# One core, attention with random features and an MLP: ones matmuls pinned to TensorE's front, queue order and PSUM banks searched anew

## The chip, the cores and the metric

The kernel runs on one core of one Trainium2 chip. The metric is the device time of one execution in microseconds (us), all phases included; less is better. PE is the matmul engine (TensorE), DVE the vector engine, ACT the scalar engine, POOL GpSimd, and SP the engine that here does nothing but issue transfers. Each engine works through its own queue in a fixed order, and waits on semaphores for the others.

## The reference

Two parts, one after the other. Attention works on 64 pairs of batch and head with 576 positions of 64 numbers and 128 features; the MLP works on the 4608 rows that come out of it.

```
q_s, k_s = q * scale, k * scale                      # q, k, v: 8 x 8 x 576 x 64
phi(x): h = x @ omega.T - sum(x*x)/2
        return exp(h - max(h)) / sqrt(128)           # 576 x 128
q_p, k_p = phi(q_s), phi(k_s)
kv  = k_p.T @ v                                      # 128 x 64
z   = sum over positions of k_p
out = (q_p @ kv) / (q_p @ z + 1e-6)
x   = out as 4608 x 512                              # heads side by side
h   = x @ w_in                                       # 512 x 2048
y   = (h * sigmoid(h)) @ w_out                       # 2048 x 512
```

## The kernel before

**Windows of attention.** The 64 pairs are taken two at a time, in 32 *windows*, numbered 0 to 31. A window loads its keys and queries (`load_raw` and `load_nat`, lines L420 to L430) and values (`load_v`, L434). PE projects them on omega: `project` (L465 for windows 0 to 3, L470 for 4 to 7, L474 for the rest) and `project_mid`, `project_mids` for the middle rows (L486, L488, L493). In windows 0 to 3 the projection also reads the squares of the inputs, which ACT makes (`square_raw`, L448). DVE takes maxima (L503, L505, L509) and makes of them the shifts `nb` and `nbm` (L512, L513); exponentials are made on ACT (L533, L538) with parts of the subtraction on DVE (L545, L549, L554, L556). PE makes `kv` (L599), turns it (`kv_turn`, L607), sums the keys to `z` (L591); DVE makes the denominators (`denom`, L623, L629); POOL divides (`normal`, L634, and by DVE at L586 for windows 9 to 11).

**Two ways to turn the queries.** The divided features have to be transposed before the last product `numer` (L678). In 17 windows PE does it (`turn`, L657, copied by ACT at L661). In the 15 windows of `CROSS` (13 to 15 and 20 to 31) a transfer does it: ACT splits the words into two planes of 16 bits (`planes`, L642), SP issues a DMA transpose (`cross`, L646), and ACT joins the planes again (`words`, L651).

**The MLP.** Every product of the MLP is one helper, `thrice` (L848): a high and a low part of each operand, three matmuls. Weights are prepared once, kept in device memory and loaded from there in pieces `w` (512 KB; L830, L835, L840, L844) into a ring of seven buffers; operands `ts` are split into a high part by ACT (L890) and a low part by DVE (L894); sums of results are DVE's (`deep_add`, L940; `c_add`, L967), with results stored from `c` at L970 and L973. POOL makes sums and low parts of weights (L762, L781, L789, L812). MLP products begin while attention still runs; from about 580 us on PE has hardly anything else.

**What sets the order.** All work is recorded as *units* by `add(name, engine, ...)`, 3649 of them, and issued in one global order that a table of numbers gives, `RANK`, one number per unit. An engine's queue is its own units in that order. PSUM has three pools, `att` (2 banks), `acc` (4) and `h` (2); a second table, the string `HOMES`, says from which pool each unit of PE takes its banks.

```
    def run(self):
        order = sorted(zip(RANK, self.units.values()), key=lambda x: x[0])
        homes, done = iter(HOMES), set()
        for _, u in order:
            assert done.issuperset(u["after"]) and done.issuperset(u["order"]), u["name"]
            u["pools"] = [{"a": "att", "c": "acc", "h": "h"}[next(homes)] for _ in range(u["banks"])]
```

A transfer thus stands where `RANK` puts it in SP's queue, and everything behind it in that queue waits until SP has issued it. One unit computes nothing that is used: `warm` (L397) multiplies a tile of ones with itself, eight matmuls of 128x128, into a bank of its own. It waits for the tile of ones alone, which DVE writes at L385.

```
    def warm(ps):
        for _ in range(WARM):
            nc.tensor.matmul(ps[:, :P], ones.bitcast(F32), ones.bitcast(F32), start=True, stop=True)
    add("warm", "PE", 3.4, -9, warm, banks=1, free=[bk("warm")])
```

Of the kernel before, what the change touches and what calls it, by code (L numbers as in the profile page):

```python
# [39 lines left out]
BOTH = tuple(range(22, 32))  # L40
# [100 lines left out]
class Plan:  # L141
# [221 lines left out]
def attention_mlp(ctx: ExitStack, tc: tile.TileContext, qX, kX, qS, kS, qT, kT, qn, kn, v, om_in, w_in, w_out, out):  # L363
# [635 lines left out]
    for n in range(NWIN):  # L999
        calm = n < LEAD  # L1000
        fold = n in FOLD
        rows = {}
        for i, who in enumerate("kq"):
# [4 lines left out]
            def prev(s):  # L1008
# [3 lines left out]
                order=prev("raw") + ([("raw", n, "k")] if i else [("raw", n - 1, "q")] if n else []), alloc=[("in", ("in",) + w)], lat=1.1)  # L1012
# [4 lines left out]
            else:  # L1017
                before = [("nat", n, "k")] if i else ([("nat", n - 1, "q")] if n and n - 1 not in FOLD else [])
                add(("nat",) + w, "SP", 0.42, at(n, i - 13.5, 8.1 + 10 * i - 32), lambda n=n, who=who: load_nat(n, who),
                    order=before + [("raw",) + w], lat=0.95)  # L1020
# [564 lines left out]
```

## Time and profile before

| what | before |
|---|---|
| device time, median of 3 runs | 944.0 us (943.92, 944.0, 946.3) |
| the profiled execution: its time, and the span from first to last instruction | 945.41 us, 943.6 us |
| PE busy | 923.0 us (98%) |
| DVE busy | 736.3 us (78%) |
| ACT busy | 679.8 us (72%) |
| POOL busy | 384.1 us (41%) |
| mean clock granted to PE | 0.999 |
| bytes moved | 245.14 MB |

The time of an execution is 1.8 us more than the span of the profiled one. A share of busy time is a mean over the whole span, and PE's 98% leaves 20.6 us in which it does nothing: before the first matmul, in waits, and after the last.

### The profile page before, as it was taken

The numbers are of one execution on the slowest core, as the hardware profiler recorded it, in microseconds if no ns is written. First come the engines' busy times: TensorE is split into PE (matmuls) and PEld (weight loads), VectorE is DVE, ScalarE is ACT, GpSimd is POOL, SyncE is SP. The second block draws the span as 40 slices with busy tenths as digits, with TensorE's granted clock in tenths as the row PEclk, the third lists the DMA queues.
The fourth block names the chain that finished last, engine by engine and source line by source line (L and its number), as shares of the span: only waits on it lengthen the run. The fifth ranks groups of instructions, "written<-read, shape, count | busy, mean of one in ns | idle before, by whom it ended". The sixth has DMA issues, their size and how long they took to land.

```text
span 943.6 us, 16346 instructions
## 1 busy us (share of the span) xinstructions
PE 923.0 (98%) x5577; PEld 747.7 (79%) x5577; DVE 736.3 (78%) x1633; ACT 679.8 (72%) x1199; POOL 384.1 (41%) x430
## 2 busy tenths in 40 slices
PE   7999999999999999999999999999999999999998
PEld 6888887877778777777877877778878887888886
DVE  5887775797766698768998998898999974468865
ACT  7998895668987876888699897886667555114642
POOL 3775666785868556756233234322120210000000
PEclk9999999999999999999999999999999999999999
DMA  7769899998899998859968578897766575567662
GB/s 245 206 221 357 295 345 332 308 350 266 313 321 311 309 360 250 312 197 345 327 221 303 160 266 258 264 263 257 217 199 202 184 262 192 198 209 238 214 222 90
DMA packets 138258, 245.14 MB, mean 260 GB/s; under 512 B 48704, under 2 KB 79552, under 8 KB 138176
## 3 DMA queue, kind: packets, MB, share of 16 engines
q1 hardware_dynamic: 138176, 244.10, 77.7%
q8 instruction: 45, 0.74, 0.3%
q14 instruction: 37, 0.30, 0.1%
HBM read 191.17 MB, written 44.04 MB: 249 GB/s over the span
## 4 chain that ended last, share of the span: by engine, by line
PE 85%; ACT 6%; DVE 4%; DMA 3%; issue 1%; POOL 0%; SPq 0%; DVEq 0%; ACTq 0%; POOLq 0%
PE ps_acc L848 56%; PE ps_h L848 13%; PE ps_att L599 2%; ACT f L538 2%; PE ps_h L474 1%; PE ps_att L678 1%; PE ps_acc L474 1%; PE ps_att L474 1%; DMA out<-c 1%; DMA f<-f 1%; PE ps_acc L599 1%; PE ps_acc L465 1%; PE ps_att L470 1%; PE ps_acc L678 1%; DVE prod L623 1%
## 5 line engine op out<-in xcount | busy, mean ns | idle before, releaser
L848 PE MATMUL ps_acc<-ts,w 128*128 128x512 f32 x2544 | 597.6, 392 | 3.2 <-DVE ts L894 1.2
L848 PEld LDWEIGHTS ps_acc<-ts,w 128*128 128x128 f32 x2544 | 472.3, 188 | 104.4 <-DVE ts L894 2.0
L894 DVE TENSOR_TENSOR ts<-g,ts 128x1024 fp32r<-128x1024 f32 x112 | 144.2, 1297 | 38.7 <-ACT ts L890 38.5
L890 ACT CAST ts<-g 128x1024 fp32r<-128x1024 f32 x112 | 117.2, 1058 | 76.5 <-PE ps_acc L848 65.6
L848 PE MATMUL ps_h<-xq,w 128*128 128x512 f32 x576 | 141.1, 394 | 0.0
L848 PEld LDWEIGHTS ps_h<-xq,w 128*128 128x128 f32 x576 | 106.1, 188 | 21.4
L940 DVE TENSOR_TENSOR g<-ps_acc,g 128x512 f32<-128x512 f32 x144 | 93.6, 682 | 24.1 <-PE ps_acc L848 23.6
L634 POOL TENSOR_TENSOR f<-f,rd 128x384 f32<-128x384 f32 x87 | 82.8, 975 | 63.6 <-DVE rd L629 51.2
L568 POOL TENSOR_TENSOR t<-hk 128x256 f32<-128x256 f32 x64 | 48.8, 778 | 141.3 <-ACT hk L538 73.1
L886 DVE TENSOR_TENSOR g<-g,g 128x1024 f32<-128x1024 f32 x64 | 79.2, 1256 | 0.2
L582 POOL TENSOR_TENSOR es<-t,es 128x256 fp32r<-128x256 f32 x32 | 29.3, 914 | 86.0 <-ACT es L578 85.3
L762 POOL TENSOR_TENSOR w<-g,w 128x512 fp32r<-128x512 f32 x32 | 42.8, 1347 | 32.4 <-ACT w L758 23.4
L944 ACT ACTIVATE g<-g 128x1024 f32<-128x1024 f32 x36 | 37.2, 1056 | 16.4 <-DVE g L940 16.3
L623 DVE CUSTOM_DVE_ANT_0 prod<-f,ps_att 128x128 f32<-128x128 f32 (+1 forms) x130 | 37.1, 286 | 14.4 <-PE ps_att L591 6.0
L651 ACT COPY f<-f 128x2304 uint16<-128x2304 uint16 x15 | 42.5, 2835 | 4.2 <-DMA f<-f 4.2
L574 POOL TENSOR_TENSOR t<-t,hk 64x128 f32<-64x128 f32 x64 | 37.4, 584 | 14.2 <-ACT hk L533 10.1
L967 DVE TENSOR_TENSOR c<-ps_acc,c 128x512 f32<-128x512 f32 x48 | 31.6, 683 | 14.1 <-PE ps_acc L848 12.4
L623 DVE CUSTOM_DVE_ANT_0 prod<-f,ps_acc 128x128 f32<-128x128 f32 (+1 forms) x110 | 31.4, 286 | 11.8 <-ACT ic L816 4.7
L906 ACT CAST ts<-xq 128x1024 fp32r<-128x1024 f32 x21 | 22.1, 1058 | 25.0 <-PE ps_acc L848 23.4
L443 DVE TENSOR_REDUCE sq<-in 128x9 f32<-128x576 f32 x48 | 34.9, 738 | 3.1 <-ACT in L438 3.1
L910 DVE TENSOR_TENSOR ts<-xq,ts 128x1024 fp32r<-128x1024 f32 x21 | 26.2, 1246 | 14.2 <-ACT ts L906 14.2
L474 PE MATMUL ps_att<-oms,in 64*128 64x128 f32 x280 | 35.9, 279 | 0.9 <-ACT f L538 0.8
(208 smaller groups left out, 1535.6 us busy)
## 6 DMA issues: line engine op xcount, KB each, us to landing
w<-w_d SPq DMA_DIRECT2D x168, 512.0 KB, 5.4
w<-ws_d SPq DMA_DIRECT2D x48, 512.0 KB, 4.5
v<-v SPq DMA_DIRECT2D x32, 320.0 KB, 5.5
out<-c SPq DMA_DIRECT2D x17, 512.0 KB, 5.1
in<-kT SPq DMA_DIRECT2D x24, 352.0 KB, 5.6
g<-w_in SPq DMA_DIRECT2D x16, 512.0 KB, 5.5
g<-w_out SPq DMA_DIRECT2D x16, 512.0 KB, 6.1
w_d<-w SPq DMA_DIRECT2D x16, 512.0 KB, 6.5
```

Of the source, the lines that this page charges most:

```text
L474: nc.tensor.matmul(ps[:, cols], T["raw", n, who][r, o : o + P], oms[r], start=True, stop=True)
L568: nc.gpsimd.tensor_tensor(t[:, i], e[:, 5 * i : 5 * i + 2], e[:, 5 * i + 2 : 5 * i + 4], ALU.add)
L574: nc.gpsimd.tensor_tensor(t[r, i - 3, 0], t[r, i - 3, 0], e[r, MID], ALU.add)
L623: nc.vector.tensor_tensor_reduce(out=prod[r], in0=e[r, c], in1=z[r, j * M : (j + 1) * M], scale=1.0, scalar=GUARD, op0=ALU.mult, op1=ALU.a ...
L634: nc.gpsimd.tensor_tensor(e[:, c], e[:, c], rd[:, c].unsqueeze(2).broadcast_to([P, 3, M]), ALU.mult)
L651: nc.scalar.copy(en.bitcast(U16).rearrange("p (n b) -> p b n", b=2), halves)
L762: nc.gpsimd.tensor_tensor(lo, T["w", i], hi.bitcast(F32), ALU.subtract)
L848: nc.tensor.matmul(ps, w(a), x[:, b], start=first and n == 0, stop=last and n == 2, **more)
L886: nc.vector.tensor_tensor(out, a, b, ALU.subtract)
L890: nc.scalar.copy(g[:, 0], T["g", p, SOURCE[j], u])
L894: nc.vector.tensor_tensor(g[:, 1], T["g", p, SOURCE[j], u], g[:, 0].bitcast(F32), ALU.subtract)
L940: nc.vector.tensor_tensor(to, T["q", p, chain, i], T["g", p, r, i // 2][:, i % 2], ALU.add)
```

## The change

It has three parts. The unit `warm` becomes something that the first two projections must follow (`order`), so that its matmuls stand at the front of PE's queue. All of `RANK` is another table, and so is `HOMES`. Operations, their number, their sizes and the buffers stay as they were; 15 windows still go by a DMA transpose.

```
 RANK = (
-    (one number for each of 3649 units)
+    (other numbers for the same units)
...
 HOMES = (
-    "chaccchccaachcacchcahchaccchchcchcachcahccacccahccaachccacccacchacccccachcaaaaaaahhhaaaahahaaaahahaa"
+    "caccchachcahcccchaacacchhacchcchcahccchcacccccahachccchachcaccchccccacachahaaaaaahahhhaaahaaaaahahaaa"
...
                 add(pj, "PE", 2.0 if n in BESIDE else 1.7 if fold else 0.99, at(n, 3 * i, o),
                     lambda a, b, n=n, who=who: project(n, who, a, b), banks=2, after=pj_after,
-                    order=([("proj", n - 1, "k" if n - 1 in BOTH else who)] if n else []) + ([("mids", n)] if i and not fold else []),
+                    order=([("proj", n - 1, "k" if n - 1 in BOTH else who)] if n else ["warm"]) + ([("mids", n)] if i and not fold else []),
```

**PE, the start of the program.** Before, the first rows of PE's queue are the projection of window 0's keys (the tiles: `in` holds inputs and their squares, `omr` is omega):

```order
L1578 UNCONDITIONAL_BRANCH
L465 MATMUL ps_acc<-omr,in 128x128
L465 MATMUL ps_h<-omr,in 128x128
L465 MATMUL ps_acc<-ones,in 128x128
L465 MATMUL ps_h<-ones,in 128x128
```

and `warm` stands far behind, between a middle projection of windows 4 to 7 (L488) and the turns of an earlier window:

```order
L470 MATMUL ps_att<-omn,in 128x128
L488 MATMUL ps_acc<-omn,in 128x128
L397 MATMUL ps_acc<-ones 128x128 x8
L607 MATMUL ps_acc<-ident,kt 128x128
L657 MATMUL ps_att<-ident,f 128x128 x3
L657 MATMUL ps_h<-ident,f 128x128 x3
```

After, the queue begins with it:

```order
L1578 UNCONDITIONAL_BRANCH
L397 MATMUL ps_acc<-ones 128x128 x8
L465 MATMUL ps_att<-omr,in 128x128
L465 MATMUL ps_acc<-omr,in 128x128
L465 MATMUL ps_att<-ones,in 128x128
L465 MATMUL ps_acc<-ones,in 128x128
```

The eight matmuls have moved from behind some 150 rows to the first place, and the projection takes its banks from other pools.

**SP, the transpose of window 14.** Before (L434 loads values, L708 is a store of results' rest, L801, L830 and L844 load weights, L794 stores weights):

```order
L708 DMA rest_96<-xr 128x64
L801 DMA ic<-w_d 128x1024
L794 DMA w_d<-c 128x2x256 x2
L434 DMA v<-v 128x640
L646 DMA_TRANSPOSE f<-f 128x18x128
L844 DMA w<-w_d 128x1024 x3
L434 DMA v<-v 128x640
L844 DMA w<-w_d 128x1024 x2
```

After:

```order
L434 DMA v<-v 128x640
L708 DMA rest_95<-xr 128x64
L801 DMA ic<-w_d 128x1024 x2
L844 DMA w<-w_d 128x1024 x6
L646 DMA_TRANSPOSE f<-f 128x18x128
L426 DMA in<-qT 128x576
L430 DMA in<-kn 128x576
L826 DMA ws_d<-ic 128x2x256 x2
```

Six loads of weights that came right behind the transpose, or later, now stand right ahead of it; behind it stand inputs of a later window.

**POOL, around window 11's maxima.** Before (`es` are sums of keys' features, `t` their parts, `g` and `c` weights):

```order
L568 TENSOR_TENSOR t<-hk 128x256 x2
L570 TENSOR_TENSOR t<-t 128x2x128
L574 TENSOR_TENSOR t<-t,hk 64x128 x2
L789 TENSOR_TENSOR c<-g_1292,c 128x512 x2
L781 TENSOR_TENSOR g_1440<-g_1440 128x256
L582 TENSOR_TENSOR es<-t,es 128x256
L781 TENSOR_TENSOR g_1440<-g_1440 128x256 x3
```

After:

```order
L568 TENSOR_TENSOR t<-hk 128x256 x2
L570 TENSOR_TENSOR t<-t 128x2x128
L781 TENSOR_TENSOR g_1344<-g_1344 128x256 x3
L789 TENSOR_TENSOR c<-g_1344,c 128x512 x2
L781 TENSOR_TENSOR g_1450<-g_1450 128x256 x3
L574 TENSOR_TENSOR t<-t,hk 64x128
L781 TENSOR_TENSOR g_1450<-g_1450 128x256
L574 TENSOR_TENSOR t<-t,hk 64x128
```

The same kinds of operations stand in another order, and six sums of weights (L781) and two low parts (L789) now come between the second and the third step of the keys' sums.

## Rows read from the trace of the kernel before

**Rows 1.** The page's part 1, and PE's granted clock in 40 equal slices (tenths).

```profile
PE 923.0 (98%) x5577; PEld 747.7 (79%) x5577; DVE 736.3 (78%) x1633; ACT 679.8 (72%) x1199; POOL 384.1 (41%) x430
...
PEclk9999999999999999999999999999999999999999
```

**Rows 2.** What PE waited for: total us, times, longest us.

```profile
PE ps_acc L591 <- DVE hk L556: 1.6, 1, 1.6
...
PE ps_acc L848 <- DVE ts L894: 1.2, 1, 1.2
PE ps_acc L657 <- DVE hk L545: 1.1, 1, 1.1
PE ps_acc L848 <- DMA w<-w_d: 0.9, 1, 0.9
PE ps_acc L599 <- DMA v<-v: 0.8, 1, 0.8
...
PE ps_h L678 <- ACT f L651: 0.4, 1, 0.4
```

**Rows 3.** Busy time by stretch: PE, PEld, DVE, ACT, POOL; clock; DMA.

```profile
24.00:48.00 24.00, 22.07 (x231) 18.88 (x231) 21.42 (x85) 22.16 (x54) 17.03 (x25) 1.00 0.79 211
48.00:72.00 24.00, 23.89 (x179) 20.31 (x180) 20.64 (x71) 23.35 (x56) 16.95 (x21) 1.00 0.71 228
...
580.00:938.00 358.00, 357.85 (x1814) 291.19 (x1813) 279.70 (x476) 200.42 (x240) 40.34 (x49) 1.00 0.66 215
```

**Rows 4.** PE's timeline at the start: start us, duration, instruction, [idle before].

```profile
4.83 0.58 PE L465 MATMUL ps_acc<-omr,in 64*128 64x128 f32 x1 [4.83 <-ACT omr L403]
...
5.41 0.42 PE L465 MATMUL ps_acc<-ones,in 64*128 64x128 f32 x1
...
5.63 0.42 PE L465 MATMUL ps_acc<-ones,in 64*128 64x128 f32 x1
...
8.54 0.79 PE L486 MATMUL ps_att<-omr,in 128*128 128x128 f32 x2
...
11.68 0.27 PE L465 MATMUL ps_acc<-omr,in 64*128 64x128 f32 x1
```

**Rows 5.** ACT's timeline, the squares of window 1's keys.

```profile
8.14 0.74 ACT L448 ACTIVATE in<-in 128x640 f32<-128x640 f32 x1 [1.47 <-DMA in<-kX]
```

**Rows 6.** DVE's timeline at the start.

```profile
0.83 0.17 DVE L385 MEMSET ones<- 128x128 f32 x1 [0.83 <-PEq L1572]
...
11.92 1.29 DVE L505 TENSOR_REDUCE nbk<-ps_acc 128x4 f32<-128x512 f32 x2 [1.23 <-PE ps_acc L465]
...
27.93 0.69 DVE L505 TENSOR_REDUCE nbq<-ps_acc 128x4 f32<-128x512 f32 x1 [0.93 <-PE ps_acc L465]
```

**Rows 7.** PE's timeline from 40 to 49 us, the unit `warm`.

```profile
40.99 1.95 PE L397 MATMUL ps_acc<-ones 128*128 128x128 f32 x16
```

**Rows 8.** Line L646: ns min/median/max on SP, and from issue to landing.

```profile
L646 SPq DMA_TRANSPOSE f<-f x15: 1773/2246/5782, 289.5 to 763.9; - x15
...
DMA to landing us min/median/max: 3.9/5.1/8.9
```

**Rows 9.** SP's timeline, the transpose of window 14.

```profile
314.73 5.78 SPq L646 DMA_TRANSPOSE f<-f  x1
```

**Rows 10.** The chain that ended last: start us, us, what.

```profile
206.14 3.90 DVE nbm L512
...
320.62 4.32 DMA w<-w_d
...
343.25 9.18 DMA out<-c
...
563.47 8.90 DMA f<-f
```

**Rows 11.** Tile nbm, one group: ns min/median/max, first and last start.

```profile
L512 DVE TENSOR_TENSOR nbm<-mxm,sq x24: 144/161/3892, 145.5 to 708.5; 128x2 f32<-128x2 f32 x24
```

**Rows 12.** Busy time from 206.14 to 210.03 us, columns as in rows 3.

```profile
206.14:210.03 3.89, 3.89 (x18) 3.00 (x17) 3.89 (x1) 1.07 (x2) 3.87 (x5) 1.00 1.03 384
```

**Rows 13.** Busy time from 310 to 320 us, same columns.

```profile
310.00:320.00 10.00, 10.00 (x45) 8.27 (x45) 4.16 (x6) 9.97 (x16) 3.57 (x3) 1.00 1.07 288
```

More of the change, by code (lines that the diff above doesn't have):

```diff
@@ L169 @@
 RANK = (
[183 rows of a table removed]
[183 rows of a table added]
 )
 HOMES = (
-    "chaccchccaachcacchcahchaccchchcchcachcahccacccahccaachccacccacchacccccachcaaaaaaahhhaaaahahaaaahahaa"
-    "haahaahhhaacchhacccccaacccaachaccaccacchchacaccachhccaccacacaaccacchaccaachcchcaacahaccacacaahahhcac"
-    "cahhcahchahahchcahcahchaccahaahahaaahahccaahcahccchahaahahcchccahhahahaccchhahcaachahcahahcacaaahaha"
-    "hhachcachcaahcchhchaachchaacacchahacahhcahcahhahaahahchacahhchacachaaahhch"
+    "caccchachcahcccchaacacchhacchcchcahccchcacccccahachccchachcaccchccccacachahaaaaaahahhaaahaaaaahahaaa"
+    "aahahahhhaahccahcacaacccacaccaccaaaccacchcaccccacacchcacccaccachahcahcaacccccaaacacachcacacaaaaahhaa"
+    "ahahhacahcahhahcahhaccahhhhaahahahahhaacchahcahccchahahcahachccahhahahacchahaachacaahhahahcacacahaha"
+    "hachcaachcaahchchhhaachchaachcahchaaahhahacaahahaahahchahahchaaccchhahahac"
 )
```

366 rows, old and new, of the table RANK are left out of this document.

## The prediction

> **What bounds the kernel now.** I read the page first. PE is busy 923.0 us of the span of 943.6, DVE 736.3 and ACT 679.8, and PE's granted clock shows 9 tenths or more in every slice [rows 1]. The change adds no work to PE and takes none away: the same units, the same shapes, 15 windows still turned by a transfer. So PE's 923.0 us stay, and what can move is the 20.6 us in which PE does nothing. I took those apart by the list of PE's waits and its timeline. Before the first matmul PE sits 4.83 us, until omega is there [rows 4]; after its last matmul some 4.3 us pass with the last sums and the store. The other 11.4 us are waits between, and the six that the change can touch are in [rows 2]: 1.6 and 1.1 for DVE's subtractions, 1.2 for low parts, 0.9 for a load of weights, 0.8 for values, 0.4 for a joined transpose.
>
> Then the stretches. From 24 to 48 us PE is busy 22.07 of 24, ACT 22.16, DVE 21.42: no engine alone is the bound, the three wait for each other. From 48 to 72 PE is busy 23.89 and ACT 23.35 [rows 3]. What comes earlier in the first 48 us therefore comes earlier at the end, if PE has no gap later that swallows it, and from 580 us on PE has 0.15 us of gaps [rows 3].
>
> One more fact is hidden in PE's 923.0: a slow start. The first projection's steps follow each other every 0.22 us (5.41, 5.63); it takes from 4.83 to 8.54, 3.71 us [rows 4]. The same work at full pace takes 1.88 us (the next one, from 11.68 on). The unit `warm` takes 0.12 us for each of its 16 passes at 41 us [rows 7], so the first projection ran at half that pace, as at 1.2 of the two levels 1.2 and 2.4 GHz, although the slices of [rows 1] show full clock. The half pace ended at about 9.2 us, after PE had worked without a gap since 4.83.
>
> **The change, step by step. First: `warm` to the front.** It needs only the tile of ones, which DVE has written at 1.0 [rows 6]. At half pace 16 passes take 16 x 0.22 = 3.5 us, so it is done by about 4.6, before omega is there at 4.83: it costs nothing there. At 41 us it leaves a hole of 1.95 us of PE's time [rows 7]. And the slow start falls on it: of the 4.4 us that PE worked at half pace before (4.83 to 9.2), 3.5 are now `warm`'s, and some 0.9 are left for the first projection, which then takes about 2.2 us instead of 3.71: 1.5 us earlier. (If the pace does not rise by then, the projection stays at 3.7.)
>
> Not all of that arrives. Window 1's keys are squared by ACT at 8.14 only, when their load lands [rows 5], and are ready at 8.88; their projection takes 1.88 at full pace, and so ends at about 10.8 instead of 11.68: 0.9 us. This is the part I hold for certain, as DVE works without a break from that point (11.92, [rows 6]) and it and ACT feed PE. Two waits inside this stretch may go besides, since the queues around them are in another order: DVE's 0.93 at 27.93 [rows 6] and PE's 0.8 for values [rows 2], whose load now stands earlier in SP's queue, ahead of a weight load. I count three quarters of these 1.75, 1.3 us. **Head: -2.2.** Bounds: 0, if DVE and ACT stay the bound with their own order; -6.1, if PE were it (1.95 for `warm`, 2.2 of half pace, and the 1.93 that PE lacks from 24 to 48 us, [rows 3]).
>
> **Second: transposes and the loads around them.** A transpose holds SP between 1.77 and 5.78 us, and lands 3.9 to 8.9 us after its issue [rows 8]. The long ones are those issued while other transfers fly. That of window 14 holds SP from 314.73 to 320.5 [rows 9]; the loads of weights behind it are issued from 320.62 on, the first lands 4.32 us later [rows 10], and PE waits 0.9 for it [rows 2]. The transpose at 563.47 takes 8.90 [rows 10], and PE waits 0.4 for its words. The wait of 1.2 for low parts goes back along the chain to a store that took 9.18 us at 343.25 [rows 10], in traffic, not to a transpose.
>
> After, six loads stand ahead of window 14's transpose, and PE has some 20 us of work between it and the first product that needs a load behind it, against 2 before. That removes the 0.9. The joined words now have about twice the work ahead of their user (median over the 15 windows, by durations of before), so the 0.4 should go too, and the 1.2 depends on a ring of `c` that comes round in another order: half of it. That is -1.9. On the other side, windows 20, 27 and 30 have 0 to 4 us of PE's work (again by durations of before) between their transpose and the first load needed behind it; a hold of 2.25 (the median) and a landing of 4.3 do not fit into that if the ring is not full. Before, seven windows were as tight and one of them waited, 0.9: so I add 0.5. **Transfers: -1.4.** Bounds: -2.4 (all three gone, none new) and +2.7 (each of the three waits 0.9, nothing gained).
>
> The Trainium skill speaks against this part: "Advanced Engine Details and Errata", section X-Bar Transpose (TRN2), says that transposes by DMA are as fast as other DMAs, and "DMA: Bandwidth & Descriptors", section Rules for kernel authors, that a transpose next to ordinary DMAs needs nothing. By that the part would be worth 0. [Rows 8] disagree: an issue that takes up to 5.78 us.
>
> **Third: DVE held by POOL.** Window 11's `nbm`, two numbers a row, took 3.89 us where the median of 24 is 0.161 [rows 11]. In those 3.89 us POOL was busy for 3.87 with five instructions [rows 12], one behind the other; DVE ran when they ended. It is on the chain [rows 10], and PE's two waits behind it are 1.1 and 1.6, 2.7 us. After, POOL's order there is another, but still a row of six sums and two low parts without a stop, and `nbm` stands between the same neighbours on DVE. Whether it falls into such a row is a matter of a microsecond, so I take half: **-1.3.** Bounds: 0 and -2.7; and a hold in some other window costs the same with the other sign.
>
> The Trainium skill, "SBUF — State Buffer", section SBUF: two separate sides, has DVE and GpSimd share a port that one holds for a whole instruction. By it the wait would be at most one POOL instruction, 1.27 us (the longest kind there), and the term under -1. The row shows one of 3.89.
>
> **Fourth: DVE later.** Three low parts of the MLP around 330 to 345 us stand behind 5 to 7 us more of DVE's work than before, as window 16's maxima are ahead of them. DVE had 5.84 us idle from 310 to 320 [rows 13], so most of it is covered; without that cover it would be up to 2.5 us, the 5.4 that were the smallest extra less the 2.9 that the first of them had to spare. I take +0.5 (0 to +2.5). The waits for ACT at 423 and 509 us I leave as they are.
>
> **Sum.** -2.2 - 1.4 - 1.3 + 0.5 = -4.4. The searched order will also have small waits that I can't see, as the old one had some 2 us of them (0.2 to 0.5 each); old and new cancel but for +0.4, a guess. So -4.0. The waits are those of the profiled execution, which took 945.41, 1.4 above the median of 944.0; less 4.0 it would be 941.4. I take the sum off the median: **940.0 us**.
>
> **The rivals.** A measurement of this kernel can tell about 0.3%, 2.8 us, from no change.
>
> *Only the head pays.* The transposes' holds come back elsewhere, and DVE is held by POOL in another place: 944.0 - 2.2 = 941.8. For it: three windows are tighter after, and POOL's rows are as long. Against it: the loads stand further ahead at most places, by durations of before. By the rule of the Trainium skill on transposes this is the result as well.
>
> *The front does not pay either.* Loads set the pace of the first 20 us (the wait of 1.47 in [rows 5]), the order searched anew has as many waits as the old one: 943.0 to 944.5, no change. For it: ACT and DVE are busy nine tenths of the time from 24 to 72 [rows 3], so that `warm`'s 1.95 us turn into idle time of PE. Against it: the half pace is seen in rows, and nothing but omega's arrival stands between `warm` and the first projection.
>
> *A load behind a transpose comes late (the other side).* The windows from 20 on have a transpose each. If SP stays held in 20, 27 and 30 as at 314.73, 5.78 instead of 2.25, each such window waits 5.78 + 4.32 less 4 us of work, some 6 us, unless PE's pieces in the ring cover it. One such wait beyond the head's gain makes 944.0 - 2.2 + 6 = 947.8. It decides from two transfers in flight at issue that land more than 2 us later. For it: six loads right ahead of a transpose mean a long hold, and 27 has no work at all between. Against it: a ring of seven pieces usually holds several, so that before only one window in fifteen waited.
>
> **How the numbers follow.** The forecast 0.56, its own range 936 to 941.2 (head at -4 and all waits gone, or the head alone and a little); only the head 0.20; front does not pay 0.12; a load late 0.12. The range from 935.5 to 946 leaves out a head paid by PE in full (below) and the worst of the last case (above), some 2 in 10. Faster by more than 2.8 (below 941.2): the forecast, 0.56. Within 2.8: the two next, and a quarter of the last, 0.34. Slower: 0.10.
>
> **What would show it.** The front: PE's first row is `warm` at about 1.0, its passes 0.22 apart; the first projection lasts about 2.2 us, window 1's keys are through by 10.8, and no row of ones near 41. Transfers: no wait for `w` at window 14, its hold on SP longer than 5 without a wait of PE's; shares of waits at windows 20, 27 and 30 under 1 us. POOL: the longest `nbm` below 2 us. The sum of PE's waits from 10 us on falls from 11.4 to about 7. I am wrong if PE's busy time itself changes by more than the 2 us of the slow start, if the first projection still takes 3.7, or if a wait above 2 us stands behind a transpose or a `nbm`.

## The result, and the profile after

The changed kernel takes 934.88 us (median of 4 runs, 934.62 to 935.15) against 944.97 of before (4 runs): a ratio of 0.9893, with a 95% interval of 0.9875 to 0.9910, some 10 us off. The forecast was 940.0, the range 935.5 to 946. The direction was right; the size was less than half of what came, and the time lies just below the range. The profiled execution has a span of 933.2 us where before had 943.6.

The page's first line, beside [rows 1]: the busy times of the engines are those of before to within 5 us, so all of it is idle time of PE.

```profile
PE 923.8 (99%) x5577; PEld 748.4 (80%) x5577; DVE 731.8 (78%) x1633; ACT 679.7 (73%) x1201; POOL 380.1 (41%) x430
```

What PE waited for (total us, times, longest us), to be laid beside [rows 2]:

```profile
PE ps_acc L397 <- DVE ones L385: 1.1, 1, 1.1
PE ps_att L493 <- DVE den L623: 0.9, 1, 0.9
PE ps_att L474 <- ACT f L538: 0.8, 1, 0.8
PE ps_acc L848 <- ACT f L533: 0.5, 1, 0.5
PE ps_att L493 <- ACT f L538: 0.3, 1, 0.3
PE ps_att L599 <- ACT kw L612: 0.3, 1, 0.3
PE ps_h L848 <- DVE ts L864: 0.3, 1, 0.3
```

None of the six waits of [rows 2] is there any more, no transfer ends a wait of PE's, and no wait but the first is longer than 0.9. Gone, too, is a wait of before that neither [rows 2] nor the prediction has, although it was the second longest behind omega's: for DVE's `den`, at 24 us. In PE's timeline of before:

```profile
24.06 0.37 PE L465 MATMUL ps_att<-omr,in 64*128 64x128 f32 x1 [1.46 <-DVE den L623]
```

The stretches of [rows 3], after (its last one ends ten us earlier):

```profile
24.00:48.00 24.00, 23.28 (x224) 19.05 (x221) 22.18 (x87) 23.68 (x59) 19.18 (x27) 1.00 0.69 221
48.00:72.00 24.00, 23.95 (x170) 19.37 (x169) 20.14 (x57) 23.87 (x54) 16.14 (x19) 1.00 0.71 216
...
580.00:928.00 348.00, 347.85 (x1770) 283.29 (x1769) 271.48 (x449) 192.75 (x230) 41.58 (x48) 1.00 0.67 217
```

From 24 to 48 us PE lacks 0.72 where it lacked 1.93, and ACT, which I had taken to be at its limit with 22.16 of 24, is busy 23.68. PE's timeline at the start, beside [rows 4]:

```profile
1.05 3.78 PE L397 MATMUL ps_acc<-ones 128*128 128x128 f32 x16 [1.05 <-DVE ones L385]
4.85 0.58 PE L465 MATMUL ps_att<-omr,in 64*128 64x128 f32 x1
...
5.43 0.42 PE L465 MATMUL ps_att<-ones,in 64*128 64x128 f32 x1
...
5.64 0.42 PE L465 MATMUL ps_att<-ones,in 64*128 64x128 f32 x1
...
6.54 0.27 PE L465 MATMUL ps_att<-omr,in 64*128 64x128 f32 x1
...
6.65 0.27 PE L465 MATMUL ps_att<-omr,in 64*128 64x128 f32 x1
...
7.53 0.49 PE L486 MATMUL ps_acc<-omr,in 128*128 128x128 f32 x2
```

The ones end at 4.83 and cost the projection nothing; its steps are 0.21 apart up to about 6.3 and 0.11 after that; it lasts 2.68 us instead of 3.71. Window 1's keys are squared 1.35 us earlier than in [rows 5], and DVE's first maximum of that window comes 1.66 us earlier than the 11.92 of [rows 6]. (That load's arrival varies by itself: the squares start at 6.7 to 8.2 us over the profiles here, in the old order and in the new one, so this part of the comparison is not the change's alone.)

```profile
6.79 0.74 ACT L448 ACTIVATE in<-in 128x640 f32<-128x640 f32 x1 [0.35 <-DMA in<-kX]
```

```profile
10.26 0.69 DVE L505 TENSOR_REDUCE nbk<-ps_acc 128x4 f32<-128x512 f32 x1 [1.14 <-PE ps_h L465]
```

The transposes (line L646, beside [rows 8]) hold SP for at most 3.74 us, and the median lands in 4.0:

```profile
L646 SPq DMA_TRANSPOSE f<-f x15: 1762/2035/3740, 291.8 to 762.1; - x15
...
DMA to landing us min/median/max: 3.9/4.0/5.9
```

And the longest `nbm` (beside [rows 11]) is 0.73 us:

```profile
L512 DVE TENSOR_TENSOR nbm<-mxm,sq x24: 150/161/731, 146.0 to 698.3; 128x2 f32<-128x2 f32 x24
```

Where the 10.4 us of span went, from the two profiles: PE begins 3.78 us earlier, the ones take 1.83 longer than at 41 us and the first projection 1.03 less, together -2.98; waits from 10 to 72 us fall from 3.36 to 0.61, -2.75; the two waits behind window 11's `nbm` are gone, -2.73; the 1.17 near 371 us is gone; the two that a transfer ended after 300 us (one of them by way of the joined words) are gone, -1.27; the small ones elsewhere grow by 0.8. Sum -10.1.

### The profile page after: what moved, and what is told of

Read it like the earlier page. It is cut to its first block, busy times and chain, and to the rows that moved or that the text cites. A ratio compares the mean times of both kernels' runs of the same rounds, so it can differ in the third digit from the quotient of the medians.

```text
span 933.2 us, 16362 instructions
## 1 busy us (share of the span) xinstructions
PE 923.8 (99%) x5577; PEld 748.4 (80%) x5577; DVE 731.8 (78%) x1633; ACT 679.7 (73%) x1201; POOL 380.1 (41%) x430
## 4 chain that ended last, share of the span: by engine, by line
PE 91%; ACT 3%; DVE 3%; issue 1%; DMA 1%; POOL 0%; SPq 0%; DVEq 0%; ACTq 0%
PE ps_acc L848 61%; PE ps_h L848 14%; PE ps_h L474 2%; PE ps_acc L474 2%; PE ps_att L474 2%; PE ps_att L599 1%; DVE prod L623 1%; PE ps_h L599 1%; PE ps_att L678 1%; PE ps_acc L678 1%; ACT f L538 1%; DMA rest<-xr 1%; PE ps_att L657 1%; PE ps_h L678 1%; PE ps_acc L657 1%
## 5 line engine op out<-in xcount | busy, mean ns | idle before, releaser
L894 DVE TENSOR_TENSOR ts<-g,ts 128x1024 fp32r<-128x1024 f32 x112 | 141.9, 1275 | 31.5 <-ACT ts L890 31.3
L634 POOL TENSOR_TENSOR f<-f,rd 128x384 f32<-128x384 f32 x87 | 80.5, 947 | 68.8 <-DVE rd L629 45.7
L568 POOL TENSOR_TENSOR t<-hk 128x256 f32<-128x256 f32 x64 | 52.5, 835 | 106.4 <-ACT hk L538 69.8
L582 POOL TENSOR_TENSOR es<-t,es 128x256 fp32r<-128x256 f32 x32 | 27.0, 843 | 99.5 <-ACT es L578 86.3
L623 DVE CUSTOM_DVE_ANT_0 prod<-f,ps_att 128x128 f32<-128x128 f32 (+1 forms) x140 | 40.0, 286 | 10.1 <-PE ps_att L591 4.1
L574 POOL TENSOR_TENSOR t<-t,hk 64x128 f32<-64x128 f32 x64 | 35.0, 547 | 21.2 <-ACT hk L533 17.0
L967 DVE TENSOR_TENSOR c<-ps_acc,c 128x512 f32<-128x512 f32 x48 | 31.5, 684 | 12.5 <-PE ps_acc L848 12.5
L623 DVE CUSTOM_DVE_ANT_0 prod<-f,ps_acc 128x128 f32<-128x128 f32 (+1 forms) x90 | 25.8, 286 | 12.9 <-PE ps_acc L591 5.0
L474 PEld LDWEIGHTS ps_att<-oms,in 64*128 64x128 f32 x304 | 32.4, 187 | 4.1 <-issue 3.0
```

The costliest lines, as they stand in the source:

```text
L474: nc.tensor.matmul(ps[:, cols], T["raw", n, who][r, o : o + P], oms[r], start=True, stop=True)
L568: nc.gpsimd.tensor_tensor(t[:, i], e[:, 5 * i : 5 * i + 2], e[:, 5 * i + 2 : 5 * i + 4], ALU.add)
L623: nc.vector.tensor_tensor_reduce(out=prod[r], in0=e[r, c], in1=z[r, j * M : (j + 1) * M], scale=1.0, scalar=GUARD, op0=ALU.mult, op1=ALU.a ...
L634: nc.gpsimd.tensor_tensor(e[:, c], e[:, c], rd[:, c].unsqueeze(2).broadcast_to([P, 3, M]), ALU.mult)
L894: nc.vector.tensor_tensor(g[:, 1], T["g", p, SOURCE[j], u], g[:, 0].bitcast(F32), ALU.subtract)
```

## The experiments

All edits but one change only the table of numbers (and the banks with it); a diff shows the units as they stand in the order, on the engine named. Times of the kernel before, taken beside the experiments, have medians of 944.25 to 945.36 and run from 941.25 to 952.07; the four of the changed kernel keep within 0.6 us. That difference is taken up below. Where the spread hides a term of one or two us, the verdict rests on the profile.

**The unit of ones alone, in the tables of before.** PE:

```diff
+"warm"
 ("proj", 0, "k")
...
 ("mid", 4, "k")
-"warm"
 ("ktt", 2)
```

> The tables of before, with the unit of ones alone moved to the front of TensorE's queue. Theory A (as predicted: DVE and ACT feed PE in the first 70 us, so that what PE saves turns into idle time): 0.9 to 1.5 us off, 943.5 to 944.1 against 944.97. Theory B (PE's own time bounds the start): the 1.95 us of the unit in the middle and the 1.5 us of the slow start both arrive, 3.4 off, 941.5. The body's waits at 211, 215, 325 and 371 us stay in both.

Measured: 944.18, ratio 1.0003 (0.9985 to 1.0021): no change. The 3.4 us of theory B are excluded; the 0.9 to 1.5 of theory A lie at the edge of the interval. The start is even earlier than in the changed kernel (the first projection is through at 6.88 us; 7.53 there, 8.54 in before), as the spacing of the matmuls halves at 4.3 us here and at 6.3 there. PE's timeline near 41 us, where the ones had been, shows where a part of it went:

```profile
40.18 0.55 PE L657 MATMUL ps_att<-ident,f 128*128 128x128 f32 x3 [0.99 <-POOL f L634]
40.97 0.55 PE L657 MATMUL ps_h<-ident,f 128*128 128x128 f32 x3 [0.24 <-POOL f L634]
42.26 0.52 PE L657 MATMUL ps_acc<-ident,f 128*128 128x128 f32 x3 [0.74 <-POOL f L634]
```

The turns wait 1.97 us for POOL's division: the 1.95 us of the ones had stood in front of work that was not ready. The earlier start does arrive: the wait for `den` ends at 21.99 us, where the seven profiles with the old start have it between 23.14 and 24.36, and PE still is 2.7 us earlier than in before behind window 11's `nbm` (208.68 against 211.37). Waits in the later part then take back 1.5 of it, such as one of 1.29 for low parts at 361 us that the profile of before lacks. So the time is that of theory A, but its mechanism is seen for the hole alone, and there PE waits for POOL, not for DVE or ACT.

**The same unit moved back, in the tables of after.** PE:

```diff
-"warm"
 ("proj", 0, "k")
...
 ("mid", 4, "k")
+"warm"
 ("proj", 4, "q")
```

> The tables of after, with the unit of ones alone moved back to behind window 4's middle projection. Theory A: 0.9 to 1.5 us slower than after, 935.8 to 936.4. Theory B: 3.4 slower, 938.3, with 1.95 us of ones near 35 to 40 us and a first projection of 3.7 us.

Measured: 938.19 (937.98 to 938.67), 3.3 above the changed kernel, 0.9936 (0.9914 to 0.9959) of before. In the order of after, theory B holds: there the whole of it arrives. So the order alone gives some 6 us (6.0 by the ratio, 6.6 by the medians), and the ones 3.3 on top, which they do not give without it.

**One matmul of ones instead of eight, in after.** It leaves the hole in the middle closed but gives the slow start back to the projection.

```diff
-WARM = 8
+WARM = 1
```

> After, with one matmul of ones at the front instead of eight. It leaves out nothing of the computation. The start of the first projection stays at 4.8 us, but the slow start then falls on it: 3.7 us instead of 2.3. If what comes early at the start arrives at the end in the order of after: 1.0 to 1.5 us slower than after, 936.1 to 936.4. If DVE and ACT feed TensorE there: the same time as after. So the gain of fixing the ones splits into the slow start (this run against after) and the hole in the middle (this run against the ones moved back, 938.2).

Measured: 936.71 (936.07 to 937.47), 1.8 above the changed kernel, 1.5 below the ones moved back. The first projection lasts 3.70 us again (4.71 to 8.41). So the ones' 3.3 us are about 1.8 for the slow start and 1.5 for the hole.

**Head and body exchanged.** The first 400 units of one kernel, all others in the order and banks of the other:

```diff
 RANK: units 0 to 399 as in after
-the others as in after
+the others as in before
```

> The first 400 of 3649 units (to about 65 us, the unit of ones among them) as in after, all others in the order and banks of before. If the head gave 6.0 us and the body 4.2, as the lost time of PE by stretch has it: 939.0. If the head gave only the 2.2 that were predicted: 942.8. The body's waits behind nbm and the transpose may shift, as all comes earlier.

Measured: 945.14, ratio 1.0003 (0.9983 to 1.0022). The head is the new one, with 0.6 us of waits, but at the joint, from 80 to 87 us, PE waits 2.5 us (for DVE's `xq` and `ts`), and the body's waits are all there, two of them longer: 2.0 for `w` and 1.6 for the joined words.

```diff
 RANK: units 0 to 399 as in before
-the others as in before
+the others as in after
```

> The first 400 units as in before (ones in the middle), all others in the order and banks of after. By the lost time of PE by stretch: 4.2 us off, 940.8. By the prediction's terms for the body (2.2): 942.8. If head and body don't act on each other, the gain here and in the new head with the old body add up to the whole, 10.1 us.

Measured: 939.08, ratio 0.9954 (0.9934 to 0.9974), 4.3 off by the ratio and 5.7 by the medians, although a wait of 2.4 stands at the joint. Head and body don't add up (0 and 4 to 6 against 10.1): a joint makes waits of its own. What they do show is that the body's gain is real without the new head, and larger than the 2.2 of the prediction.

**Window 14's transpose behind the loads, in before.** SP:

```diff
 ("v", 14)
-("xp", 14)
 ("w2", 0, 1, 0)
 ("w2", 0, 1, 1)
 ("w2", 0, 1, 2)
+("xp", 14)
 ("v", 15)
```

> Before, with window 14's transpose moved on SP behind the three loads of weights that followed it. If a transpose holds SP until the transfers in flight have landed (the rows of before): the loads are issued some 5.8 us earlier, the wait for w near 325 us (0.6 to 2.0 in the traces so far) is gone, about 1 us off the time. If a transpose costs what another transfer costs: the wait stays. In both, the waits at 211, 215 and 371 us stay (1.2, 1.6, 1.2).

Measured: 946.12, ratio 1.0019 (0.9998 to 1.0041). SP's timeline, beside [rows 9]:

```profile
314.56 3.02 SPq L844 DMA_DIRECT2D w<-w_d  x3
317.68 7.74 SPq L646 DMA_TRANSPOSE f<-f  x1
```

The wait for `w` near 325 us is gone as expected, but the transpose, now behind three loads of 512 KB, holds SP for 7.74 us instead of 5.78, and the time is no better. A wait of 1.65 of PE's came at 354.44. The view names ACT's squares of inputs (L438) for it, but a product reads none of them: DVE's sum L967 ended just there, at 354.34, after it had waited 1.85 for a store that took 10.8 us to land (9.18 in before). Whether the longer hold made that store late is not shown.

**The six loads behind it, in after.** SP:

```diff
-("w2", 0, 1, 0), ("w2", 0, 1, 1), ("w2", 0, 1, 2), ("w2", 0, 1, 3), ("w2", 0, 4, 0), ("w2", 0, 4, 1)
 ("xp", 14)
+("w2", 0, 1, 0), ("w2", 0, 1, 1), ("w2", 0, 1, 2), ("w2", 0, 1, 3), ("w2", 0, 4, 0), ("w2", 0, 4, 1)
 ("raw", 17, "q")
```

> After, with the six loads of weights that stand ahead of window 14's transpose moved right behind it. If the transpose holds SP: the first of them is issued only when the transpose has been issued, 318.6 plus 2 to 4 us, instead of 304 to 312; it lands about 4.3 us later, and TensorE, which wants it by about 317 us, waits 5 to 9 us: 940 to 944 against 934.9. If the transpose costs what another transfer costs, it still waits for ACT's planes at 318.6, and the six loads with it: then 5 us. Below 1 us of wait both are wrong, and the ring of seven buffers covers it.

Measured: 943.17 (941.39 to 944.36), 8.3 above the changed kernel. PE waits 5.73 us for `w` at 324.83. The transpose held SP for 2.0 only; what delayed the loads is that SP stood before it until ACT's planes were there, from 306 to 318.76. So the run does not tell the two theories apart; it prices the order of the queue. It costs more than the wait. Busy time by stretch (PE, PEld, DVE, ACT, POOL; granted clock; DMA):

```profile
319.00:324.00 5.00, 0.10 (x2) 0.00 (x0) 5.00 (x7) 1.72 (x3) 3.47 (x2) 0.72 0.90 229
324.00:326.00 2.00, 1.17 (x3) 0.98 (x4) 0.54 (x4) 0.00 (x0) 0.00 (x0) 0.50 1.01 367
326.00:328.00 2.00, 2.00 (x7) 1.52 (x6) 0.00 (x0) 0.00 (x0) 0.00 (x0) 0.50 1.02 412
328.00:330.00 2.00, 2.00 (x10) 1.67 (x9) 0.00 (x0) 0.65 (x1) 0.00 (x0) 1.00 1.05 404
```

After the idle stretch the clock is at 0.50, the lower of its two levels, 1.2 GHz, and the first matmuls are 0.43 us apart up to 328 us instead of 0.23: another 1.5 us.

**Window 11's `nbm` a little later, in before.** DVE:

```diff
+("top", 11, "q", 0)
 ("nbm", 11)
 ("low", 11, "q", 2)
...
-("top", 11, "q", 0)
```

> Before, with one maximum of the queries (0.67 us) moved on DVE ahead of window 11's nbm, which then begins 0.6 us later, in the same row of POOL's instructions. Theory 'chance' (the hold of 3.89 us is bad luck in the taking of turns): nbm takes 0.2, the two waits of 1.15 and 1.58 on TensorE fall to about 0, 2.7 off, 942.1 against 944.8. Theory 'gap' (DVE comes in only where POOL leaves a gap, and the row up to 210.01 has none): nbm still ends at about 210.0 with a hold of 3.2; only the second wait shrinks by 0.6; 944.

**A gap in POOL's row, in before.** POOL:

```diff
 ("cs", 5, 0)
+("cs", 5, 1)
 ("esl", 10)
-("cs", 5, 1)
```

> Before, with one sum of weights on POOL moved ahead of the keys' sum near 208.6 us, so that it follows the sum that it depends on and POOL leaves a gap of some 0.08 us there. Theory 'gap': window 11's nbm ends at that gap, about 208.7 instead of 210.03, a hold of 2.5 instead of 3.89; TensorE's wait of 1.15 goes and that of 1.58 falls to about 0.2, 2.5 off. Theory 'chance': a hold of any length, not at that gap.

**No hold at all, in before.** Three engines:

```diff
 DVE:
-("top", 11, "k", 1)
 ("topm", 11)
 ("nbm", 11)
+("top", 11, "k", 1)
 POOL:
+("esl", 10)
 ("co", 4, 0)
 ("co", 4, 1)
 ("cs", 5, 0)
-("esl", 10)
 ACT:
-("ch", 4, 1)
 ("esh", 10)
+("ch", 4, 1)
```

> Before, with three units moved around window 11's nbm: on DVE the nbm comes ahead of a maximum of the keys (begins 0.6 us earlier), on POOL the keys' sum, which waits for ACT, comes ahead of two low parts of weights, so that POOL stands still when nbm begins; one conversion on ACT moves with them. Theory 'gap': nbm takes 0.2 to 1.3 us, TensorE's waits of 1.15 and 1.58 at 211 and 215 us are gone, 2.7 off: the profile's wait before 220 us is that of before without them, the median 942. The wait of 1.17 near 371 us, where POOL holds a low part on DVE, stays.

Measured: 945.16, ratio 1.0000 (0.9981 to 1.0019), for the first; 944.15, 0.9996 (0.9976 to 1.0016), for the second; 941.14, 0.9975 (0.9956 to 0.9994), for the third. The row of `nbm` (ns min/median/max) in each, in this order:

```profile
L512 DVE TENSOR_TENSOR nbm<-mxm,sq x24: 144/162/3403, 144.7 to 708.2; 128x2 f32<-128x2 f32 x24
```

```profile
L512 DVE TENSOR_TENSOR nbm<-mxm,sq x24: 147/161/2511, 144.0 to 705.0; 128x2 f32<-128x2 f32 x24
```

```profile
L512 DVE TENSOR_TENSOR nbm<-mxm,sq x24: 142/161/818, 144.1 to 704.7; 128x2 f32<-128x2 f32 x24
```

Begun 0.5 us later relative to POOL's row, it is held 0.5 us less and ends at the same point of it (and PE's second wait falls from 1.58 to 0.98, as theory "gap" had it); with a gap put into the row, it ends at the gap. POOL's timeline in before, piece by piece around the hold (206.14 to 210.03), then with the gap, where `nbm` runs from 204.65 to 207.16:

```profile
206.64 1.28 POOL L789 TENSOR_TENSOR c<-g,c 128x512 fp32r<-128x512 f32 x1
207.89 0.73 POOL L781 TENSOR_TENSOR g<-g 128x256 f32<-128x256 f32 x1
208.58 0.74 POOL L582 TENSOR_TENSOR es<-t,es 128x256 fp32r<-128x256 f32 x1
209.28 0.73 POOL L781 TENSOR_TENSOR g<-g 128x256 f32<-128x256 f32 x1
210.09 0.73 POOL L781 TENSOR_TENSOR g<-g 128x256 f32<-128x256 f32 x1
```

```profile
206.40 0.74 POOL L781 TENSOR_TENSOR g<-g 128x256 f32<-128x256 f32 x1
207.22 0.75 POOL L781 TENSOR_TENSOR g<-g 128x256 f32<-128x256 f32 x1
```

Independent instructions of POOL begin 0.03 to 0.04 us before the last one ends (206.64 + 1.28 is past 207.89), and DVE does not get in; one that needs the result of the last begins 0.08 us after its end (209.28 + 0.73 = 210.01, next at 210.09), and there DVE does. Theory "gap" holds. The hold of 3.89 us is in every kernel with the old order here but these three (the ones at the front, the new head, the loads first), so it is no accident. The price was as in the prediction: with the hold gone, both waits behind it are gone and the time is 2.4 lower by the ratio (0.6 to 4.2 by its interval), 3.1 by the medians (941.14 against 944.25). The second kernel lost 1.15 of PE's waits only: the other one stayed at 1.6, as PE came earlier too, which I had not expected. The times of the first two show none of the 0.6 and 1.15 us, which the spread would hide.

**Three loads out of a transpose's way, in the kernel without the hold.** SP, and ACT's square of one of the loads behind the joining:

```diff
-("w2", 1, 3, 2), ("raw", 28, "q"), ("nat", 28, "q")
 ("xp", 24)
+("w2", 1, 3, 2), ("raw", 28, "q"), ("nat", 28, "q")
 ACT:
-("sq", 28, "q")
 ("rc", 24)
+("sq", 28, "q")
```

> The kernel without window 11's hold (941.1; before with three units moved), with three loads (one of weights, two of window 28's queries) moved on SP from ahead of window 24's transpose to behind it, and the square that needs one of them moved on ACT behind the joining of the planes. There the transpose held SP for 7.01 us near 558 us, landed later still, and TensorE waited 2.03 for the joined words near 571 us. If a transpose lasts until the transfers in flight have landed: its hold falls to 2 to 3 us, it lands 4 to 5 us after its issue, the wait near 571 is gone, 0.5 to 2 us off the time. If transposes cost the same with and without traffic: hold and wait stay.

Measured: 941.26, ratio to before 0.9951 (0.9926 to 0.9977), where the kernel without the hold had 941.14 and 0.9975 (0.9956 to 0.9994): the intervals overlap, and no gain is shown. The transpose in SP's timeline, first without and then with this edit:

```profile
558.05 7.01 SPq L646 DMA_TRANSPOSE f<-f  x1
```

```profile
560.08 1.81 SPq L646 DMA_TRANSPOSE f<-f  x1
```

It lands 3.92 us after its issue instead of 10.58, and the wait of 2.03 near 571 us is gone. So the hold and the late landing come from the loads in flight. What they cost in time is not shown: the span of both profiles is 939.7, as this execution has waits of 1.30 and 0.32 at 359 and 320 us that the other lacks.

**PE's last waits filled, in after.** PE:

```diff
+("pr", 0, 5, 4)
 ("proj", 18, "k")
...
-("pr", 0, 5, 4)
...
+("deep", 1, 0, 7)
 ("mids", 20)
...
-("deep", 1, 0, 7)
```

> After, with two units of the MLP moved forward into TensorE's longest waits that are left: one product (1.4 us) ahead of window 18's projection (waits of 0.84 and 0.34 near 413 us), one of the next level (1.4 us) ahead of window 20's middle projection (0.9 near 433 us). If their operands are there in time, up to 2.1 us off: 932.8 to 934. If the low parts that they need come later than 412 and 432 us, the wait only changes its name: 934.9.

Measured: 938.63 (937.92 to 939.76), 3.8 slower than after. PE's timeline:

```profile
413.34 0.37 PE L474 MATMUL ps_att<-oms,in 64*128 64x128 f32 x1 [0.83 <-ACT f L538]
...
415.67 1.65 PE L848 MATMUL ps_acc<-ts,w 128*128 128x512 f32 x6 [0.70 <-ACT f L661]
418.45 0.52 PE L657 MATMUL ps_acc<-ident,f 128*128 128x128 f32 x3 [0.45 <-ACT kw L612]
419.54 0.50 PE L591 MATMUL ps_acc<-es,ones 128*128 128x256 f32 x2 [0.57 <-ACT f L661]
```

The wait for ACT stayed where it was, and three others for ACT came behind it (for copies of turns and for `kw`), as ACT's own order had not moved with PE's. No version here beats the changed kernel.

## Why the prediction was wrong, point by point

**The head was the term most off: -2.2 said, about -5.7 measured** (-2.98 for the start and the ones, -2.75 for the waits to 72 us). The start itself went as predicted: ones at 1.05, done before omega, no ones near 41. The projection took 2.68 instead of the 2.2 said, as I had the end of the half pace wrong: in before, the matmuls of 9.13 and 9.34 us are still 0.21 apart, and only those from 10.01 on are 0.11 apart.

Two steps failed. The first is "Not all of that arrives": I took DVE's and ACT's unbroken work in [rows 3] for a limit that no order can pass, and one arrival of window 1's keys (8.14 us, which varies from 6.7 to 8.2) for a fixed point, and kept 0.9. In the order of after the ones' whole worth arrives: 3.3 us when undone, 1.8 for the slow start and 1.5 for the hole. In the order of before the ones alone bring no change, so the small sum was right there, but not its reason: the early start is still there at 208 us, and the hole is lost to POOL's division. A share of busy time of nine tenths on two engines told of the old queues, not of a bound: ACT is at 23.68 of 24 now.

The second is the list of "the six that the change can touch": it leaves out, without a reason, PE's wait of 1.46 us for `den` at 24.06, and counts in its place 0.93 us of DVE's idle time at 27.93. The new order has no wait there, and that is more than half of the 2.75. The bound on the other side, -6.1, was the better value, though it has not this wait either.

**POOL and DVE: -1.3 said, -2.73 for this place.** The mechanism was right, the half was not. I called it "a matter of a microsecond" whether `nbm` falls into such a row. It is a matter of order: with the old one the hold stands at 3.89 in each kernel that leaves that place as it was, and with the new one in none. And my reading of the new row was wrong: "a row without a stop" of dependent sums does have gaps. In the changed kernel, `nbm` at 202.84 takes 0.23 us in the middle of such sums: one ends at 203.04, the next begins at 203.12.

**A wait was put to the wrong cause.** I led the 1.2 for low parts near 371 us [rows 2] back to a store that took 9.18 us. The DVE instruction that it waits for took 2.28 us, where one takes 1.22 elsewhere, and POOL had begun the first of two instructions, one of 1.31 us, 0.11 us before it (the view puts both into one row):

```profile
368.95 2.28 DVE L894 TENSOR_TENSOR ts<-g,ts 128x1024 fp32r<-128x1024 f32 x1 [2.33 <-ACT ts L890]
```

```profile
368.84 3.55 POOL L805 TENSOR_TENSOR ic<-ic 128x512 f32<-128x512 f32 x2
```

PE's wait is between 1.15 and 1.18 in all eight kernels with the old order there, while DVE's wait for the store, before its sum L967, varies from 0.9 to 1.8. That speaks for the hold and against the store, but it was read from timelines: no run took this hold away by itself. If it is right, POOL's holds were worth 3.9 of the 4.3 us by which PE's waits after 72 us fell.

**Transfers: -1.4 said; -1.27 for the two waits named, and none of the +0.5 that windows 20, 27 and 30 were to cost.** In sum close, by luck: the 1.17 moved to the line above. The mechanism held: a transpose issued with loads in flight lasts until they have landed (7.01 against 1.81 us, 10.58 against 3.92 to landing). In before, eight of 15 were issued with transfers in flight for more than 1.2 us, and in seven of these the hold ends within 0.2 us of the last landing; in after it is six, and the longest hold is 3.74. Window 14's did not take the more than 5 us that I forecast: it was issued at 318.58, when all but one of the transfers ahead of it had landed. It took 3.11 with the last landing 0.98 behind its issue, which this mechanism does not explain. The rule of the Trainium skill that spoke against it ("Advanced Engine Details and Errata", X-Bar Transpose (TRN2)) holds here, as to landing, for most transposes with nothing in flight: 3.9 us, where a load of `w` takes 3.2 at the least and 5.0 in the median. It does not hold for one in traffic. The other sentence of the Trainium skill that the prediction set beside it ("DMA: Bandwidth & Descriptors", Rules for kernel authors) stands there beside corrupted results and says nothing of time.

**DVE later: +0.5 said, 0 measured.** No wait for DVE's low parts stands between 326 and 371 us in after.

**Of the rivals** none happened. The one in which the 1.95 us of the ones turn into idle time of PE is what the ones alone did in the old order. Loads put behind a transpose did come late when forced, 8.3 us slower, and the new order avoids it; but there SP waited for ACT's planes, and the transpose itself held it for 2.0, so the rival's size of 6 us was right by luck.

**What stays open.** The spread of the kernel before is not explained. Some of its PE waits differ among the profiles that have its order there (0 to 2.0 at 325 us for `w`, 0 to 1.3 near 360 for low parts, 0 to 2.0 near 571 for joined words), and so does the start (the wait for `den` ends between 23.14 and 24.36); these are one profile for each of several kernels, and they fit a range of 10 us only in part. None of the changed kernel's PE waits ends with a transfer, and its four times lie within 0.6 us; the six loads behind the transpose, which make such a wait, brought a range of 3.0 back. But the old head with the new body has no such wait in its profile either, and its times range over 6.9 us, so transfers on PE's path are not shown to be the cause. How much of the order's 6 us each of its thousands of moves gave can't be said beyond the terms above.

## What to carry to other kernels

A kernel whose times vary by 1% has a single profile that is one of many. Here some waits stood at the same length wherever the queues around them were left alone (about 1.2 us at 211 and 371, 1.6 at 215), and those for loads varied, so look at several profiles before one wait is given a price. Go through the whole list of waits, too: the one left out here was longer than all but one of those counted. Work that is moved out of a queue gains only what the next instructions in it were ready for, so a move and the order around it are judged together (0 us in one order, 3.3 in the other), and an engine that is nine tenths busy in one order is not thereby the limit of the next. Where SP issues transposes, count what is in flight at that moment, as the hold grows with it, and what stands behind them, as it also waits until the transpose's own operand is there.

## What the runs showed of the hardware

At window 11's `nbm`, DVE was kept out not for one instruction of POOL's but until POOL left a gap: 3.89, 3.40 and 2.51 us, each ending with a POOL instruction that was followed by a dependent one. All other holds in the profile of before (54 instructions of DVE that took over 0.25 us longer than the median of their kind) are below 1.1 us. The Trainium skill ("SBUF — State Buffer", SBUF: two separate sides) has a lock for a whole instruction; those 54 are short enough for it, and the one that mattered is not. And an idle stretch of PE cost twice: 5.73 us of waiting were followed by 1.5 us lost at the lower clock level.
